# Score tiles of four blocks per head, filling a PSUM bank, in place of three, in an attention and MLP kernel

## Chip, cores, metric

One core of a Trainium2 chip. The metric is the device time of one execution in microseconds (us); a kernel's time is the median of several executions.

## The reference

For 8 batches: grouped attention (16 query heads, 4 key heads, 384 positions, 64 dimensions a head), then a residual MLP block on the 384 x 1024 result.

```python
scores = q @ k.T / 8                       # per head, 384 x 384, softmax over keys
x   = softmax(scores) @ v                  # heads side by side: 384 x 1024
tok = w_tok @ (alpha1 * x + beta1)
u   = x + lam * tok
out = u + lam * (relu((alpha2 * u + beta2) @ w_ch1) @ w_ch2)   # 1024 -> 4096 -> 1024
```

## The kernel before

The attention of batch b+1 (a "side", a list of small units) is woven into the MLP of batch b (`main`), so that TensorE is never without work. Batch 0's attention has no MLP to hide in and runs first, alone: the prologue. The softmax needs no maximum, and its sum comes out of the av matmul as a 65th column.

A score tile is one pair of heads `p` times one block of keys `sk`: 384 queries, three blocks of 128, for two heads. The heads have 64 dimensions each and lie on the two halves of the partitions, so the two matmuls use half of TensorE's rows each and run side by side (below: the half-row mode; a group of such matmuls in a row is one visit to it). They write two PSUM banks of 512, and use 384 of each.

```python
def scores(p, sk):
    hk = (2 * p) // G
    sc = psum.tile([P, 2, 512], f32, tag="sc", name="sc", bufs=2)
    for hh in range(2):
        r = slice(hh * D, (hh + 1) * D)          # 64 of the 128 rows
        nc.tensor.matmul(out=sc[:, hh, :S]..., lhsT=kT[r, sk, hk, :], rhs=qT[r, :, p, :], ...)
    e = sb.tile([P, 2, S], bf, tag="es", name="es", bufs=6)
    nc.scalar.activation(out=e, in_=sc[:, :, :S], func=EXP, scale=scale_qk)
    ess[p, sk] = e

def scores2(j):                                  # one unit of a woven side: two tiles
    scores(*divmod(2 * j, NST))
    scores(*divmod(2 * j + 1, NST))
# ... av_piece(p, hh): 9 matmuls with es as weights; on hh == 1 a VectorE chain
#     (reciprocal, two multiplications, a1f, a). tok(p), a2_transpose(p) follow.
```

`main(b)` yields after every 4 matmuls, and the loop that drives it then issues the next unit when its turn has come. An h tile is 8 matmuls of 384 columns; even tiles are evicted by ScalarE (relu), odd ones by VectorE; two PSUM buffers.

The softmax here doesn't subtract the row's maximum and nothing guards it: scores larger than these inputs give would overflow.

## Time and profile before

833.53 us median of three runs. The profiled execution splits by where the first and last h matmuls of each batch stand:

| stretch | us |
|---|---|
| prologue, to the first h | 49.28 |
| batch 0's MLP with side 1 | 104.75 |
| six batches with sides 2 to 7, each | 98.27 |
| batch 7's MLP alone, and the end | 87.9 |

The lines of the page, of stretches of the span and of the timeline are in the prediction.

### The profile page before, as it was taken

The numbers are of one execution on the slowest core, as the hardware profiler recorded it, in microseconds if no ns is written. First come the engines' busy times: TensorE is split into PE (matmuls) and PEld (weight loads), VectorE is DVE, ScalarE is ACT, GpSimd is POOL, SyncE is SP. The second block draws the span as 40 slices with busy tenths as digits, with TensorE's granted clock in tenths as the row PEclk, the third lists the DMA queues.
The fourth block names the chain that finished last, engine by engine and source line by source line (L and its number), as shares of the span: only waits on it lengthen the run. The fifth ranks groups of instructions, "written<-read, shape, count | busy, mean of one in ns | idle before, by whom it ended". The sixth has DMA issues, their size and how long they took to land.

```text
span 831.5 us, 13628 instructions
## 1 busy us (share of the span) xinstructions
PE 806.4 (97%) x5768; PEld 438.2 (53%) x5819; DVE 350.8 (42%) x728; ACT 224.1 (27%) x335; POOL 187.2 (23%) x229
## 2 busy tenths in 40 slices
PE   6789999999999999999999999999999999999997
PEld 3555554555455554556445564556545555456543
DVE  3855652244453434434343443433444344352211
ACT  4525520333104322043212332033320442202100
POOL 5504441123202250022400224012410221003000
PEclk9969999999999999999999999999999999999999
DMA  9999999799959997499917999389995999119711
GB/s 233 193 156 174 200 211 192 142 174 172 105 104 137 179 169 76 99 172 175 164 37 148 165 180 129 80 131 176 180 84 110 127 179 145 35 48 178 100 39 38
DMA packets 265341, 115.06 MB, mean 138 GB/s; under 512 B 113728, under 2 KB 258496, under 8 KB 265280
## 3 DMA queue, kind: packets, MB, share of 16 engines
q0 software_dynamic: 200832, 83.28, 88.2%
q1 hardware_dynamic: 63488, 30.13, 15.8%
q10 hardware_dynamic: 960, 0.79, 0.4%
q8 instruction: 45, 0.74, 0.4%
q14 instruction: 16, 0.13, 0.0%
HBM read 172.56 MB, written 12.58 MB: 223 GB/s over the span
## 4 chain that ended last, share of the span: by engine, by line
PE 94%; DMA 3%; DVE 1%; issue 1%; ACT 0%; POOL 0%; DVEq 0%; POOLq 0%
PE h L328 41%; PE ch L352 40%; PE sc L180 4%; PE av L198 4%; PE tok L224 3%; DMA a2T<-a 2%; DMA q_raw<-in_q_dram 1%; PE tp L168 0%; ACT hT L336 0%; DVE a L229 0%; PE tp L239 0%; PE tp L249 0%; DVE x L211 0%; DVE a1f L214 0%; DVE g L204 0%
## 5 line engine op out<-in xcount | busy, mean ns | idle before, releaser
L328 PE MATMUL h<-a2T,w 128*128 128x384 bf16 (+1 forms) x2048 | 363.2, 328 | 1.5 <-ACT hT L336 1.4
L352 PE MATMUL ch<-w,hT 128*128 128x512 bf16 x1485 | 346.3, 379 | 2.7
L328 PEld LDWEIGHTS <-w 128*128 128x128 bf16 x2048 | 190.9, 98 | 135.7 <-issue 22.6
L126 POOL DMA_DIRECT2D w<-in_moe_w_ch_dram x128 | 112.3, 878 | 556.8 <-PE sc L180 273.5
L183 ACT ACTIVATE es<-sc 128x768 bf16<-128x768 f32 x192 | 145.0, 808 | 311.2 <-PE sc L180 311.2
L352 PEld LDWEIGHTS <-hT 128*128 128x128 bf16 x1536 | 143.2, 98 | 161.9 <-issue 7.6
L338 DVE TENSOR_SCALAR hT<-h,bias 128x384 bf16<-128x384 f32 x128 | 79.0, 617 | 160.4 <-PE h L328 159.9
L336 ACT ACTIVATE hT<-h,bias 128x384 bf16<-128x384 f32 x128 | 74.5, 582 | 205.4 <-PE h L328 188.6
L357 DVE TENSOR_TENSOR o<-ch,lam 128x512 f32<-128x512 f32 x48 | 33.1, 690 | 142.5 <-PE ch L352 142.5
L227 DVE TENSOR_TENSOR x<-tok,x 128x384 f32<-128x384 f32 x64 | 35.6, 556 | 79.5 <-PE tok L224 79.5
L198 PEld LDWEIGHTS <-es 128*128 128x128 bf16 x1152 | 53.0, 100 | 22.3 <-issue 2.4
L198 PE MATMUL av<-v,es 128*128 128x65 bf16 x1152 | 57.9, 196 | 0.0
L180 PE MATMUL sc<-qT,kT 64*128 64x384 bf16 x384 | 51.7, 338 | 2.7 <-ACT es L183 2.1
L224 PE MATMUL tok<-a,wtokT 128*128 128x128 bf16 x576 | 44.3, 224 | 5.8 <-POOL a L217 3.0
L224 PEld LDWEIGHTS <-wtokT 128*128 128x128 bf16 x576 | 38.8, 100 | 17.4 <-issue 5.7
L211 DVE TENSOR_TENSOR x<-av,rinv 128x192 f32<-128x192 f32 x128 | 39.8, 352 | 2.3
L229 DVE TENSOR_TENSOR a<-x,al 128x384 bf16<-128x384 f32 x64 | 38.0, 593 | 2.7 <-DMA a2T<-a 0.6
L214 DVE TENSOR_TENSOR a1f<-x,g 128x384 f32<-128x384 f32 x64 | 35.7, 558 | 2.4
L208 DVE RECIPROCAL rinv<-av 128x6 f32<-128x6 f32 x64 | 12.3, 192 | 51.7 <-PE av L198 51.4
L358 DVE TENSOR_TENSOR o<-o,x 128x512 f32<-128x512 f32 x48 | 33.3, 694 | 1.6
L217 DVE TENSOR_TENSOR a<-a1f,h 128x384 bf16<-128x384 f32 x58 | 32.3, 557 | 2.2
L180 PEld LDWEIGHTS <-kT 64*128 64x128 bf16 x384 | 12.3, 95 | 36.3 <-issue 35.1
(38 smaller groups left out, 131.6 us busy)
## 6 DMA issues: line engine op xcount, KB each, us to landing
w<-in_moe_w_ch_dram POOLq DMA_DIRECT2D x135, 512.0 KB, 6.4
out_dram<-o SPq DMA_DIRECT2D x48, 256.0 KB, 2.1
q_raw<-in_q_dram POOLq DMA_DIRECT2D x21, 256.0 KB, 9.4
kst<-in_k_dram SPq DMA_DIRECT2D x16, 192.0 KB, 2.7
w<-in_moe_w_ch_dram POOLq DMA_DIRECT2D x10, 256.0 KB, 10.0
w<-in_moe_w_ch_dram POOLq DMA_DIRECT2D x1, 2048.0 KB, 35.4
v<-in_v_dram POOLq DMA_DIRECT2D x21, 64.0 KB, 8.8
a2T<-a SPq DMA_TRANSPOSE x53, 4.3
```

The lines of the kernel that those rows point to most:

```text
L126: nc.gpsimd.dma_start(out=t, in_=w1src[:, :, c * CW * P:(c + 1) * CW * P])
L180: nc.tensor.matmul(out=sc[:, hh, :S].rearrange("p (st s) -> p st s", st=NST), lhsT=kT[r, sk, hk, :], rhs=qT[r, :, p, :], start=True, stop= ...
L183: nc.scalar.activation(out=e, in_=sc[:, :, :S], func=EXP, scale=scale_qk)
L198: nc.tensor.matmul(out=av[:, hh, sq, :], lhsT=ess[p, sk][:, hh, sq * P:(sq + 1) * P], rhs=vb[:, sk, hk, :], start=(sk == 0), stop=(sk == N ...
L211: nc.vector.tensor_tensor(out=x[:, :, c0:c0 + D], in0=av[:, hh, :, :D], in1=rinv[:, hh].to_broadcast([P, NST, D]), op=MUL)
L214: nc.vector.tensor_tensor(out=t, in0=x[:, :, cols(p)], in1=bc(g1, p), op=MUL)
L224: nc.tensor.matmul(out=ps[:, tt, :], lhsT=wtokT[:, st, tt * P:(tt + 1) * P], rhs=a1s[p][:, st, :], start=(st == 0), stop=(st == NST - 1))
L229: nc.vector.tensor_tensor(out=a2s[p], in0=u, in1=bc(al2, p), op=MUL)
L328: nc.tensor.matmul(out=ps[:, :n], lhsT=w1[:, dt, j * P:(j + 1) * P], rhs=a2T[:, dt, :n], start=(dt == 0), stop=(dt == NDT - 1))
L336: nc.scalar.activation(out=hT[:, nt, :], in_=ps[:, :S], func=RELU, bias=c1)
L338: nc.vector.tensor_scalar(out=hT[:, nt, :], in0=ps[:, :S], scalar1=c1, scalar2=0.0, op0=ADD, op1=mybir.AluOpType.max)
L352: nc.tensor.matmul(out=ps, lhsT=hT[:, nt, ms * P:(ms + 1) * P], rhs=w2[:, nt, cs], start=(nt == 0), stop=(nt == NNT - 1))
```

## The change

A side's 72 blocks of 128 x 128 per head are numbered through, and four in a row make a run that fills a bank for each of the two heads. A unit issues two runs, so a side visits the half-row mode 9 times in place of 12, and has 18 exps of 1024 columns in place of 24 of 768. A run crosses from one key block to the next once, so it is cut into two matmuls per head. The second run's exp is put off until main next stands in the middle of a tile, so that a relu can pass.

```diff
-        def scores(p, sk):
-            ...
+        def scores(i, later=False):
+            sc = psum.tile([P, 2, 4, P], f32, tag="sc", name="sc", bufs=2)
+            k = 4 * i
+            while k < 4 * i + 4:
+                n = min(4 * i + 4, k - k % NST + NST) - k
+                p, sk, st = k // (NST * NST), k // NST % NST, k % NST
+                for hh in range(2):
+                    r = slice(hh * D, (hh + 1) * D)
+                    nc.tensor.matmul(out=sc[:, hh, k % 4:k % 4 + n], lhsT=kT[r, sk, 2 * p // G, :],
+                                     rhs=qT[r, st:st + n, p, :], start=True, stop=True)
+                k += n
+            def exp():
+                e = sb.tile([P, 2, 4, P], bf, tag="es", name="es", bufs=EB)    # EB = 4
+                nc.scalar.activation(out=e, in_=sc, func=EXP, scale=scale_qk)
+                ess[i] = e
+            if later: late.append(exp)
+            else: exp()
         def scores2(j):
-            scores(*divmod(2 * j, NST))
-            scores(*divmod(2 * j + 1, NST))
+            scores(2 * j)
+            scores(2 * j + 1, True)
 ...  # the woven side: 9 groups instead of 12, 37 units (4 of them empty) instead of 36
 ...  # the prologue's units, in a new order:
         add(k_transpose, 0)
         add(q_transpose, 0)
-        for p in range(NP):
-            add(scores, p, 0)
-            ...
+        for i in range(18):
+            add(scores, i)
+            if i == 1:
+                add(q_transpose, 1)
+            ...
 ...  # the loop over main's yields:
+                half = not half
+                if late and half:
+                    late.pop(0)()
```

More of the change, by code (lines that the diff above doesn't have):

```diff
@@ L57 @@
     RING = 5
+    EB = 4
     scale_qk = 1.0 / float(D) ** 0.5
@@ L134, in tp_ps @@
         return psum.tile(shape, bf, tag="tp", name="tp", bufs=1)
+    late = []
     xs = {}
@@ L173, in q_transpose @@
                                   in_=ps.rearrange("p (a st) s -> p a st s", a=2))
-        def scores(p, sk):
-            hk = (2 * p) // G
-            sc = psum.tile([P, 2, 512], f32, tag="sc", name="sc", bufs=2)
-            for hh in range(2):
-                r = slice(hh * D, (hh + 1) * D)
-                nc.tensor.matmul(out=sc[:, hh, :S].rearrange("p (st s) -> p st s", st=NST),
-                                 lhsT=kT[r, sk, hk, :], rhs=qT[r, :, p, :], start=True, stop=True)
-            e = sb.tile([P, 2, S], bf, tag="es", name="es", bufs=6)
-            nc.scalar.activation(out=e, in_=sc[:, :, :S], func=EXP, scale=scale_qk)
-            ess[p, sk] = e
+        def scores(i, later=False):
[13 more added lines that the diff above has]
+                ess[i] = e
+            if later:
+                late.append(exp)
+            else:
+                exp()
         def scores2(j):
-            scores(*divmod(2 * j, NST))
-            scores(*divmod(2 * j + 1, NST))
+            scores(2 * j)
+            scores(2 * j + 1, True)
         def av_piece(p, hh):
+            while late:
+                late.pop(0)()
             if hh == 0:
@@ L197, in av_piece @@
                 for sk in range(NST):
-                    nc.tensor.matmul(out=av[:, hh, sq, :],
-                                     lhsT=ess[p, sk][:, hh, sq * P:(sq + 1) * P],
+                    k = (p * NST + sk) * NST + sq
+                    nc.tensor.matmul(out=av[:, hh, sq, :], lhsT=ess[k // 4][:, hh, k % 4, :],
                                      rhs=vb[:, sk, hk, :], start=(sk == 0), stop=(sk == NST - 1))
@@ L268, in side @@
                 add(q_transpose, 1)
-            for j in range(NP * NST // 2 + 4):
-                if 2 * j < NP * NST:
-                    add(scores2, j)
-                if pe_flip and j in (1, 4):
-                    add(q_transpose, 2 + j // 4)
-                for p in range(NP):
-                    last = (NST * p + NST - 1) // 2
-                    if last == j - 1:
-                        add(av_piece, p, 0)
-                        add(av_piece, p, 1)
-                    if last == j - 3:
-                        add(tok if pe_flip else tok_flip, p)
-                    if pe_flip and last == j - 4:
-                        add(a2_transpose, p)
-                    if pe_flip and j > 12:
-                        add(lambda: None)
+            for j in range(NP + 4):
+                if 1 < j < NP + 2:
+                    add(av_piece, j - 2, 0)
+                    add(av_piece, j - 2, 1)
+                if j <= NP:
+                    add(scores2, j)
+                    if pe_flip and j in (1, 3):
+                        add(q_transpose, 2 + j // 2)
+                if 2 < j < NP + 3:
+                    add(tok if pe_flip else tok_flip, j - 3)
+                if pe_flip and j > 3:
+                    add(a2_transpose, j - 4)
+                if j < 2:
+                    us.extend([lambda: None] * 2)
             return us
@@ L287, in side @@
         add(q_transpose, 0)
-        for p in range(NP):
-            add(scores, p, 0)
-            if p == 2:
-                add(k_transpose, 2)
-            add(scores, p, 1)
-            if 0 < p < 4:
-                add(q_transpose, p)
-            if p > 0:
-                add(av_piece, p - 1, 0)
-            if p == 2:
-                add(wtok_transpose)
-            if p > 2:
-                add(tok_flip if p < NP - 1 else tok, p - 3)
-            add(scores, p, 2)
-            if p > 0:
-                add(av_piece, p - 1, 1)
+        for i in range(18):
+            add(scores, i)
+            if i == 1:
+                add(q_transpose, 1)
+            if i in (5, 9):
+                add(q_transpose, i // 4 + 1)
+            if i == 4:
+                add(k_transpose, 2)
+            if i == 6:
+                add(wtok_transpose)
+            for p in range(NP):
+                last = (9 * p + 8) // 4
+                if i == last + 1:
+                    add(av_piece, p, 0)
+                    add(av_piece, p, 1)
+                if i == last + 2 and p > 1:
+                    add(tok_flip, p - 2)
         add(tok, NP - 3)
-        add(a2_transpose, NP - 4)
         add(av_piece, NP - 1, 0)
@@ L411 @@
             us = side(b + 1) if b + 1 < B else []
+            half = False
             done, t, loaded, flipped = 0, 0, b + 2 >= B, b + 2 >= B
@@ L417 @@
                 t += dt
+                half = not half
+                if late and half:
+                    late.pop(0)()
                 if done < len(us) and done * t_all * span < len(us) * (t - t_all * lead):
```

## The prediction

> **What bounds the kernel now.** The page comes first: which engine is full, when, and what the chain that ended last is made of.
>
> ```profile
> PE 806.4 (97%) x5768; PEld 438.2 (53%) x5819; DVE 350.8 (42%) x728; ACT 224.1 (27%) x335; POOL 187.2 (23%) x229
> ...
> PE   6789999999999999999999999999999999999997
> ...
> PEclk9969999999999999999999999999999999999999
> ...
> PE h L328 41%; PE ch L352 40%; PE sc L180 4%; PE av L198 4%; PE tok L224 3%; DMA a2T<-a 2%; DMA q_raw<-in_q_dram 1%; PE tp L168 0%; ACT hT L336 0%; DVE a L229 0%; PE tp L239 0%; PE tp L249 0%; DVE x L211 0%; DVE a1f L214 0%; DVE g L204 0%
> ```
>
> The TensorE is the bound, and the scores are 4% of the chain: the change works on some 33 us of 831 there. A busy TensorE need not be an efficient one, so I read starts below, not busy times. Next, stretches of the span (columns: busy time and count of each engine, granted clock, DMA):
>
> ```profile
> 14.00:26.00 12.00, 10.52 (x97) 7.32 (x97) 7.41 (x18) 4.75 (x6) 1.99 (x2) 1.00 1.37 268
> 26.00:40.00 14.00, 10.08 (x144) 6.48 (x144) 13.22 (x28) 9.75 (x13) 8.70 (x9) 1.00 1.38 189
> 40.00:49.30 9.30, 5.15 (x55) 4.61 (x55) 7.84 (x20) 0.96 (x2) 0.92 (x2) 0.52 1.84 174
> 49.30:154.00 104.70, 104.33 (x769) 56.79 (x773) 49.02 (x123) 31.49 (x50) 33.94 (x43) 0.98 1.40 185
> 154.00:743.60 589.60, 585.95 (x4231) 316.07 (x4272) 250.07 (x504) 161.88 (x240) 121.31 (x146) 1.00 1.03 132
> ```
>
> There are two regimes. Up to 49.3 us the attention of batch 0 runs alone, and from 26 us on VectorE is the full engine there (13.22 of 14.00 us). After that, each batch's MLP runs with the next batch's attention woven in, and TensorE is over 99% busy: six such batches in 589.6 us, 98.27 us each. Batch 7's MLP has nothing woven in. So seven attention sides stand directly on TensorE's time, and one stands in a VectorE-bound prologue.
>
> The timeline of TensorE in the first woven batch shows what a score group costs (start, length, line, count):
>
> ```profile
> 157.27 0.50 PE L180 MATMUL sc<-qT,kT 64*128 64x384 bf16 x4
> 157.70 2.12 PE L328 MATMUL h<-a2T,w 128*128 128x384 bf16 x12
> 159.75 0.50 PE L180 MATMUL sc<-qT,kT 64*128 64x384 bf16 x4
> 160.19 2.77 PE L328 MATMUL h<-a2T,w 128*128 128x384 bf16 x16
> 162.79 0.44 PE L198 MATMUL av<-v,es 128*128 128x65 bf16 x9
> 163.07 2.11 PE L328 MATMUL h<-a2T,w 128*128 128x384 bf16 x12
> ```
>
> Lengths overlap, so I use starts. Sixteen h matmuls before an av take 162.79 - 160.19 = 2.60 us, 0.1625 each, with no cost of changing over. Twelve before a score group take 159.75 - 157.70 = 2.05 us instead of 1.95: 0.10 lost on entry. The group itself lasts 0.43 us, though its two pairs (two heads side by side on half the rows) need only 2 x 0.1625 = 0.325 at the h rate; 0.11 is lost in it and on exit. A group thus costs **0.54 us, of which about 0.21 is the change of mode**. Twelve groups per side make 6.4 us.
>
> A second loss shows once per batch:
>
> ```profile
> 196.55 0.44 PE L198 MATMUL av<-v,es 128*128 128x65 bf16 x9
> 196.82 2.11 PE L328 MATMUL h<-a2T,w 128*128 128x384 bf16 x12
> 197.02 0.20 DVE L208 RECIPROCAL rinv<-av 128x6 f32<-128x6 f32 x1 [1.61 <-PE av L198]
> ...
> 198.98 0.61 DVE L338 TENSOR_SCALAR hT<-h,bias 128x384 bf16<-128x384 f32 x1
> ...
> 199.61 0.32 PE L328 MATMUL h<-a2T,w 128*128 128x384 bf16 x1 [0.24 <-ACT hT L336]
> ```
>
> This av piece was issued in the middle of an odd h tile. Its VectorE chain stands ahead of that tile's eviction, which ends at 199.59, and the h matmul that reuses the PSUM buffer starts 0.02 later. The profile names ACT as the releaser, but VectorE ended last. From start to start I count about 0.31 us here and 0.08 at another place: some 0.39 per batch.
>
> **What the Trainium skill says.** "TensorEngine Tiling (Array Packing)", Key Properties: changing the tiling mode, not just the tile, drains the engine. The trace agrees: 0.21 us per visit to the half-row mode, nothing for av. "TensorE: Matmul & The Clock Gate", Part 3, has tiles of different row groups run at once, about 4 ns apart; here the two heads of a pair start 3 to 4 ns apart, and the next pair 170 later. "ScalarE: Activation LUTs", What ACT_TABLE_LOAD costs, gives 186 ns + 0.833 ns per column for immediate scale and bias; the trace's 768-column exp lasts 808 ns, so 640 + 168, close. "PSUM — Partial Sum Buffer", The four PSUM rules: one matmul output stays in a bank of 512 fp32. The old score tile fills 384 of 512; the new run of 4 x 128 fills the bank, so the same two banks per buffer hold a third more. The page's rule agrees with the shapes; the trace cannot show the limit itself.
>
> **The change part by part.**
>
> (1) Mode changes: two runs of four blocks per head are issued together, so a side has 9 groups in place of 12. That is 3 x 0.21 = 0.63 us less per side.
>
> (2) Columns: 72 blocks per head pass either way, 24 x 384 before and 18 x 512 after. No change.
>
> (3) Pieces: a run crosses a kT block once, so it is always cut in two (3+1, 2+2 or 1+3 blocks): 36 pairs per side for 24. The trace puts a pair's step at 0.170 to 0.173 us against 0.1625 for one h matmul, so a pair costs some 0.01 more than its columns. The smallest pair streams 128 columns, 0.054 us at the h rate, while av streams 9 load-and-multiply steps in 0.27 us, 0.03 each; two weight loads should just about fit. I take 0.005 to 0.015 for each of 12 extra pairs: 0.06 to 0.18 more per side, say 0.12.
>
> Group after: 0.21 + 1024 x 0.1625/384 (0.433) + 0.02 = 0.66 us. Side after: 9 x 0.66 = 5.9, against 6.4: **0.5 us less per side, 3.5 us for seven.**
>
> (4) Exps: 18 of 1024 columns, 168 + 853 = 1.02 us each as an estimate from the row above, against 24 of 0.808. ScalarE has a third of its time busy or less in the woven batches: worth nothing by itself. The second exp of a group is put off for a half tile so that a relu can go between; without that, two exps in a row would block for 2.0 us (now 1.5). I counted at which half tile each unit falls: no relu comes out late.
>
> (5) Placing: the side now has 37 units instead of 36, so the phases against odd and even h tiles change. By the code's spacing the second av piece of pair 3 moves off its odd tile, but that of pair 2 falls in the middle of tile 23, odd again. Its eviction ends 2.77 us after the av's end (as above), and h wants the buffer after 1.95 us plus a score group of 0.66: 0.15 us lost, against 0.39 before. Gain 0.24 per batch, 1.4 for six; 0.3 more from batch 0's MLP, whose trace has three such gaps, 0.6 together.
>
> (6) Prologue. Its first av now needs runs 0 to 2, and the second q transpose, which waits for a load until 14.05 us, stands before run 2; the first reciprocal moves from 16.2 to about 17.4. The wtok transposes now come after the second av. Walking the new order with the old durations, I get the third reciprocal at 27.0 instead of 28.25, but the first tok's two VectorE steps after it instead of before: both orders have the same VectorE work done at 29.6. From there VectorE sets the pace with the same work. Net 0, uncertain by 1.5.
>
> Sum: -3.5 - 1.4 - 0.3 + 0 = -5.2, so 833.5 becomes **828.3 us**, 0.6% faster.
>
> **Rivals.**
>
> *The short pairs cost more than they save.* If two loads don't hide under 128 columns, or a piece must wait for its row group, each extra pair costs perhaps 0.05: 12 x 0.05 x 7 = 4.2 us more than nothing, instead of the 0.8 that I count, and the time stays near 832. For: a pair already pays 0.01. Against: av's loads stream at 0.03 and kT's next loads start 0.01 after a matmul's start.
>
> *A new wait at the PSUM or VectorE boundary.* Groups take both score buffers at once, and tok shares them; a put-off exp or a tok eviction in the way would hold TensorE in order. For: half the slack is gone. Against: a unit comes every 2.5 us, and the next group comes several units later. A stall of 0.3 in each of 9 groups would cost 19 us over seven sides; I see no chain that long. A stall of 0.3 once a batch costs 2: about 830.5.
>
> *The prologue turns.* VectorE-bound with TensorE's clock half throttled (0.52 from 40 us on), it could move 2 us either way: 826 to 831.
>
> *Scores cost nothing beyond columns* is the favourable rival: were the 0.10 on entry hidden anyway, (1) would give half, 2 us less gain.
>
> **Range and chances.** Score arithmetic is good to about 1.5 us, placing to 1.5, prologue to 1.5; together some 2.6. The surprises are rather on the slow side. Predicted 828.3, range 825.0 to 832.2. Two per cent would be 16.7 us: over a third of the 45 us that the seven sides' score groups cost in all, so 2% faster is out of reach short of a big prologue gain, and 2% slower needs a wait in every group. Faster 0.01, same 0.97, slower 0.02.
>
> **What would show it.** The period of a woven batch falls from 98.27 to about 97.5 us. Score groups number 9 a side, with 8 matmuls and about 0.66 us from the last h before to the next h. Exps last about 1.02 us, 144 of them. The wait of h on evictions shrinks but stays. The first h starts at 49.3 within 1.5. The prediction is wrong if the 128-column pairs step well above 0.065 us, if sc waits for es in the woven batches, or if the first h moves by more than 2 us.

## More of the kernel before

The queue of SyncE takes, in this order, batch 1's k, which waits until the buffers of batch 0's k have been read, and then four broadcasts:

```python
place_k(0, 0)
# ...
load_k(1)                                        # SyncE's queue: its second half waits for place_k(0, 1)
for t, ap in ((g1, moe_alpha1), (lam_t, moe_lam), (h1, moe_beta1)):
    bcast(nc.scalar, t, ap, 0, 256)
    bcast(nc.sync, t, ap, 256, DM)               # SyncE's queue, behind load_k(1)
# ...
for i, f in enumerate(side(0)):
    f()
    for g, *a in loads.get(i, []):
        g(*a)
    if i == 4:
        place_k(0, 1)                            # VectorE casts the second half of k
```

More is needed here. First the exps, from the page, and two multiplications of the prologue that read the broadcasts of lam and beta1, from VectorE's timeline:

```profile
L183 ACT ACTIVATE es<-sc 128x768 bf16<-128x768 f32 x192 | 145.0, 808 | 311.2 <-PE sc L180 311.2
...
25.14 1.26 DVE L204 TENSOR_TENSOR g<-g,lam 128x768 f32<-128x768 f32 x1
26.32 0.94 DVE L205 TENSOR_TENSOR h<-h,lam 128x768 f32<-128x768 f32 x1
```

Then SyncE's queue in the prologue (start, length until the last of the group was issued, line, transfer, count):

```profile
4.61 4.36 SPq L86 DMA_DIRECT2D kst<-in_k_dram  x2
9.02 0.95 SPq L116 DMA_DIRECT2D g<-in_moe_alpha_dram  x1
10.02 0.43 SPq L116 DMA_DIRECT2D lam<-in_moe_lam_dram  x1
10.49 0.57 SPq L116 DMA_DIRECT2D h<-in_moe_beta_dram  x1
```

The second half of the k load goes out at about 8.6 us, after the cast that frees its buffer, and the broadcasts of alpha1, lam and beta1 right behind it.

## The result

830.38 us median of four runs (828.97 to 830.79), against 833.97 for the kernel before (833.42 to 834.5): a ratio of 0.9954, with a 95% interval of 0.9937 to 0.9971. A ratio is the mean time of one kernel's fast runs over that of the other's of the same rounds, so not quite the ratio of the medians. By the threshold of 2% that is the same time; the interval shows a small real gain. The time lies in the range, 2.1 us above the prediction.

The profiled executions, split as before:

| stretch | before, us | after, us | difference | predicted |
|---|---|---|---|---|
| prologue, to the first h | 49.28 | 52.04 | +2.76 | 0 |
| batch 0's MLP with side 1 | 104.75 | 104.04 | -0.71 | -0.8 |
| six batches with sides 2 to 7 | 589.60 | 584.82 | -4.78 | -4.4 |
| batch 7's MLP alone, and the end | 87.9 | 87.9 | 0 | 0 |

The woven part does slightly more than was predicted of it, 97.47 us a batch; the whole of the miss is in the prologue. The page after, TensorE's busy time, granted clock, the chain, the exps and the scores:

```profile
PE 797.1 (96%) x5958; PEld 445.9 (54%) x6011; DVE 350.9 (42%) x728; ACT 219.0 (26%) x287; POOL 187.6 (23%) x229
...
PEclk7869999999999999999999999999999999999999
...
PE 92%; DMA 3%; DVE 2%; issue 1%; ACT 1%; POOL 0%; SPq 0%; DVEq 0%; POOLq 0%
...
L194 ACT ACTIVATE es<-sc 128x1024 bf16<-128x1024 f32 x144 | 141.2, 1021 | 302.9 <-PE sc L188 302.9
...
L188 PE MATMUL sc<-qT,kT 64*128 64x384 bf16 (+2 forms) x576 | 46.5, 278 | 0.7 <-DVE qT L175 0.7
```

An exp of 1024 columns takes 1021 ns, as estimated. The clock of the first slice is lower than before, and TensorE's share of the chain fell by two points, to VectorE and ScalarE: a first sign of the prologue. The timeline of TensorE in a woven batch after:

```profile
163.32 0.61 PE L188 MATMUL sc<-qT,kT 64*128 64x128 bf16 x8
163.87 6.67 PE L344 MATMUL h<-a2T,w 128*128 128x384 bf16 x40
170.38 0.43 PE L217 MATMUL av<-v,es 128*128 128x65 bf16 x9
```

A group of 8 matmuls lasts 163.87 - 163.32 = 0.55 us from its first start to the next h. With 0.096 of entry (the trace's starts: 258 ns from the last h, of which 162 are its own) a group costs 0.65 us. In the trace's own starts a pair of 128 columns steps by 53 ns, of 256 by 106 and of 384 by 159; only the first pair and the first h after the group take 10 ns more. So the extra cuts cost nothing that the trace can resolve.

Now the prologue. First SyncE's queue after:

```profile
4.63 11.94 SPq L87 DMA_DIRECT2D kst<-in_k_dram  x2
16.63 0.46 SPq L117 DMA_DIRECT2D g<-in_moe_alpha_dram  x1
17.14 0.42 SPq L117 DMA_DIRECT2D lam<-in_moe_lam_dram  x1
17.61 0.43 SPq L117 DMA_DIRECT2D h<-in_moe_beta_dram  x1
```

Then VectorE's timeline after, the start of the cast of k and the two multiplications that read lam and beta1 (in square brackets the idle time before, and what ended it):

```profile
15.44 0.74 DVE L95 CAST k<-kst 128x384 bf16<-128x384 f32 x2
...
25.98 0.96 DVE L222 TENSOR_TENSOR g<-g,lam 128x768 f32<-128x768 f32 x1 [2.32 <-DMA lam<-in_moe_lam_dram]
27.23 0.96 DVE L223 TENSOR_TENSOR h<-h,lam 128x768 f32<-128x768 f32 x1 [0.29 <-DMA h<-in_moe_beta_dram]
```

The broadcasts go out some 7 us later, and VectorE, which sets the pace from here, waits 2.61 us for them. Before, the same two ran at 25.14 and 26.32 without a wait.

### The profile page after: what moved, and what is told of

Same layout as the page of the kernel before. It is cut to its first block, busy times and chain, and to the rows that moved or that the text cites. A ratio compares the mean times of both kernels' runs of the same rounds, so it can differ in the third digit from the quotient of the medians.

```text
span 828.8 us, 13904 instructions
## 1 busy us (share of the span) xinstructions
PE 797.1 (96%) x5958; PEld 445.9 (54%) x6011; DVE 350.9 (42%) x728; ACT 219.0 (26%) x287; POOL 187.6 (23%) x229
## 4 chain that ended last, share of the span: by engine, by line
PE 92%; DMA 3%; DVE 2%; issue 1%; ACT 1%; POOL 0%; SPq 0%; DVEq 0%; POOLq 0%
PE h L344 41%; PE ch L368 40%; PE av L217 4%; PE sc L188 4%; PE tok L242 4%; DMA q_raw<-in_q_dram 1%; DMA h<-in_moe_beta_dram 1%; DMA a2T<-a 1%; DVE a L247 1%; ACT hT L352 0%; DVE x L229 0%; DVE x L245 0%; DVE a1f L232 0%; PE tp L171 0%; PE tp L257 0%
## 5 line engine op out<-in xcount | busy, mean ns | idle before, releaser
L344 PE MATMUL h<-a2T,w 128*128 128x384 bf16 (+1 forms) x2048 | 356.6, 327 | 1.2 <-DVE bias L350 0.2
L344 PEld LDWEIGHTS <-w 128*128 128x128 bf16 x2048 | 192.9, 98 | 129.4 <-issue 10.6
L194 ACT ACTIVATE es<-sc 128x1024 bf16<-128x1024 f32 x144 | 141.2, 1021 | 302.9 <-PE sc L188 302.9
L188 PE MATMUL sc<-qT,kT 64*128 64x384 bf16 (+2 forms) x576 | 46.5, 278 | 0.7 <-DVE qT L175 0.7
L188 PEld LDWEIGHTS <-kT 64*128 64x128 bf16 x576 | 20.1, 95 | 28.0 <-issue 23.6
```

The lines of the kernel that those rows point to most:

```text
L188: nc.tensor.matmul(out=sc[:, hh, k % 4:k % 4 + n], lhsT=kT[r, sk, 2 * p // G, :], rhs=qT[r, st:st + n, p, :], start=True, stop=True)
L194: nc.scalar.activation(out=e, in_=sc, func=EXP, scale=scale_qk)
L344: nc.tensor.matmul(out=ps[:, :n], lhsT=w1[:, dt, j * P:(j + 1) * P], rhs=a2T[:, dt, :n], start=(dt == 0), stop=(dt == NDT - 1))
```

## Theory and rivals

For the **woven part**: a visit to the half-row mode costs 0.21 us beyond its columns, and a side makes 9 instead of 12; the rest is a stall on a PSUM buffer that got smaller by where units fall. Rivals: visits are free and the gain comes from fewer, larger exps or from phase alone.

For the **prologue**: `if i == 4` counts units. Unit 4 was the third score tile; it is now the second q transpose, which waits for a load until 14.3 us. Its copy stands ahead of the cast in VectorE's queue, the cast holds back batch 1's k load, and that the broadcasts behind it (theory A). Rival B: the new order of scores and av, or a colder clock, is slower by itself.

## The experiments

Before each run stands the edit, and what was expected.

**1. The cast of k one unit earlier, in the changed kernel.**

```diff
-            if i == 4:
+            if i == 3:
                 place_k(0, 1)
```

> The changed kernel with one thing moved: the cast of the second half of k is issued one unit earlier, ahead of the second q transpose, which waits for its load until 14.3 us. Theory A (the cast stuck behind that wait holds back the next k load on the SyncE queue, and the broadcasts of lam and beta1 behind it, which VectorE then waits for): the cast is at about 7.5 us, VectorE no longer waits 2.3 + 0.3 us for lam and beta1, the first h moves from 52.0 to about 49.4, the time falls by about 2.6 us to some 827.8. Rival B (the new order of scores and av in the prologue, or the colder TensorE clock, is slower by itself): first h stays within 0.7 of 52.0, time about 830.2. The woven batches keep 97.47 us in both.

827.24 us (ratio 0.9925, 0.9911 to 0.9938). The broadcasts went out at 9 to 11 us, VectorE waited for neither, and the first h came at 47.83, even 1.5 us before that of the kernel before. Part of that is the q load, which landed at 13.3 us here, at 14.0 in the kernel before and at 14.3 in the changed one. Against the changed kernel VectorE is 0.9 us ahead at the copy behind that load (14.03 and 14.97), 3.7 at the third reciprocal (24.38 and 28.11), and the first h comes 4.2 sooner. So of 4.2 us, 0.9 come from the q load, 2.8 from the stretch that held the waits, and 0.5 from the rest. The woven batches kept 97.47. VectorE's timeline of this run:

```profile
7.31 1.16 DVE L95 CAST k<-kst 128x384 bf16<-128x384 f32 x2
...
22.65 0.95 DVE L222 TENSOR_TENSOR g<-g,lam 128x768 f32<-128x768 f32 x1
23.52 0.95 DVE L223 TENSOR_TENSOR h<-h,lam 128x768 f32<-128x768 f32 x1
```

The order itself is not slower, so that half of rival B falls. The colder clock is not separated by this run: from 14 to 26 us the granted clock was 1.00 here and 0.84 in the changed kernel. But the waits of 2.61 us ended with the landing of a load, so at most the rest can be the clock's.

**2. The same delay put into the kernel before.**

```diff
-            if i == 4:
+            if i == 7:                           # behind its second q transpose
                 place_k(0, 1)
```

> The kernel before with the same cast put behind its second q transpose, as in the changed kernel. Theory A: the broadcasts land near 26 and 27 us; the kernel before reaches the two multiplications that read them at 25.1 and 26.3, so it loses about 0.9 us, first h 49.3 to about 50.2, time 834.0 to about 835. Rival B: no loss, first h 49.3.

834.6 us against 833.63 (ratio 1.0012, interval 0.9999 to 1.0025, so the time alone does not prove it); first h at 50.30, 1.0 later, with woven batches of 98.27. Theory A gave 0.9, but not all of the 1.0 is its own. VectorE's timeline of this run has one wait on lam or beta1:

```profile
27.46 0.96 DVE L205 TENSOR_TENSOR h<-h,lam 128x768 f32<-128x768 f32 x1 [0.38 <-DMA h<-in_moe_beta_dram]
```

Another 0.23 us went on the broadcast of alpha2 behind it. lam landed at 24.8, earlier than expected, and was not waited for; and the q load landed at 14.5 in place of 14.0. So the delay shows in this kernel too, with 0.6 us of waits. The first h moves between programs with the same prologue, though: 49.28 in the kernel before, 48.48 in the next experiment.

**3. The woven sides of the changed kernel, the prologue of the kernel before.**

```diff
-        for i in range(18):
-            add(scores, i)
+        for p in range(NP):
+            add(scores_old, p, 0)
             ...                                  # the old order, tiles of 384
```

Its exps go to a part of hT that is free in the prologue, for want of room.

> The changed woven sides with the prologue of the kernel before (24 score tiles of 384 columns, its order of units; its exps written to a part of hT that is free then, for want of room). Both theories: woven batches 97.47 us as in the changed kernel, first h at 49.3, time 834.0 - 5.5 = 828.5. If the gain of the woven part were an accident of phase against the prologue, the period would move back towards 98.27.

827.83 us against 833.63 (ratio 0.9925, 0.9912 to 0.9937): 5.8 less. First h at 48.48, woven batches 97.47. Experiment 1, with the new order and a q load that landed within 0.2 us of this one's, had its first h at 47.83, so the old order is not the faster one. The woven part alone is worth 5.5 us by the periods, independent of the prologue, which turned some 2 of them back into waiting.

**4. Each run of four by itself: 18 visits a side.**

```diff
             scores(2 * j)
-            scores(2 * j + 1, True)
+            late.append(lambda: scores(2 * j + 1))
```

> The changed kernel with the second run of each group (scores and exp) put off together, so that each run of four blocks is its own visit to the half-row mode: 18 visits per side in place of 9. If a visit costs 0.21 us beyond its columns: a single run 0.21 + 0.22 + 0.01 = 0.44 us, a side 18 x 0.44 = 7.9 in place of 9 x 0.65 = 5.8, period 97.5 to about 99.5, seven sides about 14 us more: 844 to 845. If visits are free and the gain came from the exps or from where units fall: period 97.5, time 830 to 831.

844.66 us (ratio 1.0131, 1.0117 to 1.0145), period (the time of one woven batch) 99.59. Columns, cuts and exps are those of the changed kernel; only the visits doubled. TensorE's timeline of this run:

```profile
159.74 0.39 PE L188 MATMUL sc<-qT,kT 64*128 64x256 bf16 x4
160.06 4.72 PE L344 MATMUL h<-a2T,w 128*128 128x384 bf16 x28
164.72 0.39 PE L188 MATMUL sc<-qT,kT 64*128 64x128 bf16 x4
165.04 0.82 PE L344 MATMUL h<-a2T,w 128*128 128x384 bf16 x4
```

Four blocks alone last 0.32 us plus 0.10 of entry, against 0.65 for eight. With the stalls that the starts show taken out (0.41 us a batch here, 0.19 in the changed kernel), nine visits more cost 99.18 - 97.28 = 1.90, **0.211 us each**; the kernel before, with three more and a stall of 0.39, gives (97.88 - 97.28) / 3 = 0.20. The runs with 9 and 18 visits have the same exps and cuts, the one with 12 has others, and one cost per visit fits all three: the rival of the exps falls.

**5. The second exp not put off.**

```diff
-            scores(2 * j + 1, True)
+            scores(2 * j + 1)
```

> The changed kernel with the second exp of a group issued right after the first, not put off by a half tile. If the putting off matters: groups that fall in the middle of an even h tile (tiles 0 and 18 in each woven batch) put 2.0 us of exp ahead of that tile's relu, which ends about 3.0 us after the group's start while h wants the buffer after 2.6; two stalls of about 0.4 us per batch, period 97.47 to about 98.3, time some 5 us more, 835 to 836. If it is ornament: period 97.47, time 830.

833.68 us (ratio 0.9992, 0.9978 to 1.0006), period 97.92: 0.45 us a batch given up, half of what was expected. The timeline of all engines at the start of a woven batch shows the stall in tile 0:

```profile
156.16 1.94 ACT L194 ACTIVATE es<-sc 128x1024 bf16<-128x1024 f32 x2 [12.65 <-PE sc L188]
...
157.99 0.59 ACT L352 ACTIVATE hT<-h,bias 128x384 bf16<-128x384 f32 x1
...
158.62 0.65 PE L344 MATMUL h<-a2T,w 128*128 128x384 bf16 x3 [0.29 <-ACT hT L352]
```

The relu of tile 0 waits for both exps and ends at 158.58; h starts 0.04 later. In tile 18 there is none: I had overlooked that a tok of 0.5 us falls between there, which gives the relu the time. Putting the exp off is worth about 2.7 us over six batches, three quarters of the whole measured gain of 3.6, or half of the woven part's 5.5.

**6. All units of the six later batches half a tile later.**

```diff
-            lead, span = (0.04, 0.82) if b == 0 else (0, 0.95)
+            lead, span = (0.04, 0.82) if b == 0 else (0.008, 0.95)
```

> The changed kernel with all units of the six later woven batches one half tile later. If the one stall left per batch (0.19 us behind the fourth group, where an av piece falls in the middle of odd tile 23) comes from the VectorE chain standing ahead of that tile's eviction: no stall, period 97.47 to 97.28, six batches 1.2 us less, 829.2. If the stall belongs to the group itself (the buffers of the score tiles, or the exps): it stays, 97.47. If the last tok's flip then comes too late for the next batch: a wait of h on the flip, period above 97.5.

829.43 us (ratio 0.9949, 0.9932 to 0.9966), not to be told from the changed kernel by time. The trace can tell: period 97.29, as expected, and no stall. In the changed kernel the stall looked like this (timeline of all engines):

```profile
191.09 0.44 PE L217 MATMUL av<-v,es 128*128 128x65 bf16 x9
...
193.05 0.56 DVE L235 TENSOR_TENSOR a<-a1f,h 128x384 bf16<-128x384 f32 x1
193.41 0.61 PE L188 MATMUL sc<-qT,kT 64*128 64x128 bf16 x8
...
193.52 0.61 DVE L354 TENSOR_SCALAR hT<-h,bias 128x384 bf16<-128x384 f32 x1
...
194.15 0.65 PE L344 MATMUL h<-a2T,w 128*128 128x384 bf16 x3
```

The eviction of odd tile 23 stands behind the av's chain and ends at 194.13; h starts at 194.15, 0.19 us after the group would have let it.

**7. Pair 0 before the q load lands.** The first experiment, and

```diff
-            if i == 1:
-                add(q_transpose, 1)
-            if i == 4:
+            if i == 3:
                 add(k_transpose, 2)
             ...                                  # av of pair 0
+            if i == 3:
+                add(q_transpose, 1)
```

> The first experiment (cast of k one unit earlier), and the second q transpose moved behind the scores and av of pair 0, the second k transpose ahead of it: all that needs no more of q than its first part runs before the load lands at about 14 us. If the prologue is set by VectorE's work after that load: about 2 us of VectorE's chain move into its idle time, first h from 47.8 to about 45.8, time 827.2 to about 825.3. If TensorE's order or the exps set it: first h stays at 47.8.

827.16 us (ratio 0.9914, 0.9901 to 0.9927). The first h came at 46.08, as expected, but batch 0's MLP took 105.68 us in place of 104.34: side 1's q transpose now stood waiting 1.6 us for batch 1's q, which had not moved. The gain turned into a new wait.

**8. Experiments 6 and 7 together.** The edits are those above.

> Both of the last two together: first h about 45.8, period 97.28, time 824.1, some 1.1% below the kernel before. If the two gains overlap, no better than the prologue edit alone (825.3).

825.63 us (ratio 0.9895, 0.988 to 0.9909): the period gain is kept, the 1.6 us of waiting are too.

**9. Then the 2 MB load of w2 behind batch 1's q and v.**

```diff
-        loads = {7: [(load_w2, 0, 0, 2)], 25: ...
-                 ... 43: [(load_v, 1, [2])]}
+        loads = {25: ...
+                 ... 43: [(load_v, 1, [2]), (load_w2, 0, 0, 2)]}
```

> The previous best (early pair 0 and the shift), with the 2 MB load of the first half of w2, which nothing reads before about 100 us, issued behind the loads of batch 1's q and v instead of ahead of them. The previous best gave 1.6 us back: with the prologue 1.7 us shorter, batch 1's q transpose now waits for its q load (lands at 55.1 us). If that load is held up by what lies ahead of it on the DMA engines: no wait there, lam and beta1 land earlier too, main of batch 0 falls from 105.3 to about 103.7, time 825.6 to about 824. If the q load is late for another reason (issued late, behind the q buffer of batch 0): the wait stays, time 825.6.

The profiled execution took 2923.23 us; four others took 823.91 to 826.79. Such a trace explains nothing of the fast runs, so the same program was run again:

> The same program as e10_w2_behind_q, whose profiled execution took 2.9 ms with every matmul some 3.8 times as long, so that its trace says nothing of the q load. In a fast run: if the q load of batch 1 was held up by the w2 load, no wait of the q transpose in the MLP of batch 0 and the time near 824; if not (four fast runs gave 823.9 to 826.8, no better than the previous best), the wait is still there, 1.5 us, or something else has taken its place.

825.06 us (ratio 0.99, 0.9884 to 0.9917). The wait for batch 1's q is gone from batch 0's MLP: its three loads landed by 43.9 us, against 54.7 in experiment 8, so the w2 load had held it up. But the time is no better than experiment 8's, within the intervals: the prologue now ends at 46.63, and the fifth h matmul waits 0.48 us for the DMA transpose of a2. This version and experiment 8, which can't be told apart, are the best here: 1.0% below the kernel before and some 0.5% below the changed one.

**10. The k load behind the broadcasts, the cast left late.**

```diff
-        load_k(1)
         for t, ap in ((g1, moe_alpha1), ...
         ...
+        load_k(1)
```

> The changed kernel with the late cast left where it is, and batch 1's k load, which waits for that cast, put behind the broadcasts on the SyncE queue. Theory A (the queue's order carries the delay from the cast to lam and beta1): broadcasts issued at about 9 to 12 us, no VectorE wait of 2.3 us for lam, first h from 52.0 to about 49, time about 827.5, as with the early cast. If the early cast helped by itself (VectorE's 0.7 us, kT earlier): VectorE still waits for lam, first h about 51.5, time 830.

833.05 us (ratio 0.9991, 0.9975 to 1.0008): both expectations missed. VectorE no longer waits for lam, so the queue did carry the delay; but now nothing held the broadcasts back, they went out at 2 to 6 us, and TensorE's waits in the prologue show what was late instead:

```profile
PE tp L171 <- DMA q_raw<-in_q_dram: 10.8, 3, 7.2
```

In three waits TensorE stood 10.8 us for batch 0's q, against 4.4 with experiment 1; the load landed at 19.1 instead of 13.3. The first h came at 53.58. The k load's wait for its buffer had also been a brake that kept the broadcasts out of the way of the q load. That early broadcasts delay the q load is shown by this one edit; how the loads shared the DMA engines was not looked at.

## Why the prediction was right, and where not

- **The mode changes (1)** were the mechanism, and 0.21 us was their size: 0.211 and 0.20 from runs with 18, 12 and 9 visits.
- **The pieces (3)** were charged 0.12 us a side and cost none within the trace's resolution: a group took 0.65 instead of 0.66, so a side saved 0.6 rather than 0.5. The rival of costly short pairs fell: the 128-column pair stepped by 53 ns.
- **The exps (4)** did their part only by being put off, as the prediction had it; experiment 5 gives 0.45 us a batch for that.
- **The placing (5)** named the stall that would remain, behind pair 2's av in tile 23, and gave it 0.15 us; it was 0.19. The gain per batch was 0.20 instead of 0.24.
- **The prologue (6)** is the step that failed. "Net 0, uncertain by 1.5" became +2.76 in the profiled run. The walk took the old times of every instruction in the new order, and with that the old issue times of the loads. It left out an action that is tied to a unit's number and not to its name: the cast of k slid from 7 to 15 us, the broadcasts behind it with it, and VectorE waited 2.61 us. By the prediction's own sign, a first h moved by more than 2 us, it was wrong in this step; the total stayed in the range because the other steps were not off as well. Experiment 1 shows the cause, experiment 10 that the queue carried it, and experiment 2 points the same way with 0.6 us. The size is less sure: over the executions that share the new prologue the first h came at 51.1 to 52.0, with the old one at 48.5 and 49.3, so about 2.5 us. The sum of the other steps was -5.2, measured -5.5.
- Of the rivals, "the prologue turns" is what happened, for a reason that it did not name. No new wait on the score buffers appeared in the woven batches.

What stays open: why the q load of the prologue lands between 13.3 and 14.5 us in programs that issue it alike, whether its 4 us of waiting could be removed, and what the colder clock cost the prologue.

## What to carry to other kernels

Where an engine is full, count how often it changes mode and measure one change from starts, not from busy times; filling the buffer that limits a visit is worth the visits saved times the cost of one. When a list of units is reordered, look for everything keyed to a position in the list: here a cast stuck behind a load cost half of what the change had earned, through two queues. And a load that seems to be only late may be in the right place, since making it early can delay the load that is needed first.

## What the Trainium skill lacked or had wrong

- "TensorEngine Tiling (Array Packing)", Key Properties, says that a change of mode drains the engine and gives no size: 0.20 to 0.21 us per visit here, both ways together, and nothing more for further pairs within a visit (53, 106 and 159 ns for 128, 256 and 384 columns).
- "TensorE: Matmul & The Clock Gate", Back-to-back issue gap, has a load-and-multiply stream at about 81 ns for 128 columns and 131 ns for 512. With a weight load for every matmul, tok (128 columns) stepped by 56 ns and ch (the MLP's second matmul, 512) by 216 ns, which is the formula that this section keeps for isolated matmuls; Part 1 of the same page gives these very steps for back-to-back ones, so the page disagrees with itself. The same page (Part 1, Seeing it yourself) knows a clock stuck at a quarter for over 50 us; one execution of experiment 9 was slow in a way that would fit this, nearly from start to end: 2923 us, h matmuls 630 ns apart (median) instead of 162.5, 3.9 times as long, with a recorded granted clock of 1.0. That it was the clock is not shown.
- No page says that of the loads waiting in one queue a blocked one can be a useful brake: with the k load out of the way, batch 0's q landed at 19.1 us instead of 13.3 (experiment 10).
